# Long convolution and GEGLU layers on one core: forward transforms of two blocks by single token groups, spaced loads, a reordered opening

## The chip, the cores and the metric

The kernel runs on one core of a Trainium2 chip. The metric is the time of one execution on the device in microseconds (us); the time before is the median of three executions. A profile is a recording of one more execution. The engines are PE (TensorE, matrix multiplication into PSUM), DVE (VectorE), ACT (ScalarE), POOL (GpSimd) and SP (SyncE); each takes its own instructions in the order in which the program lists them, and semaphores join the engines. SP and POOL also issue the DMA transfers.

## What is computed

Two equal layers over x with 2048 tokens of width 576. Each adds a gated causal convolution and then a GEGLU feed-forward part with an inner width of 4608:

```python
def _A_ref(q, k, v, shift_k, ssm_k, ssm_D):
    ...                                  # k_shift: 4-tap causal filter of k
    kv = k_shift * v
    ...                                  # y: causal convolution of kv with ssm_k (2048 taps) by FFT
    y = y + kv * ssm_D[None, None, :]
    return q * y

def _B_ref(x, w_gate, w_up, w_down):
    return (_gelu(x @ w_gate) * (x @ w_up)) @ w_down

x = A_q
x = x + _A_ref(_layernorm(x, axis=-1), A_k, A_v, A_shift_k, A_ssm_k, A_ssm_D)
x = x + _B_ref(_layernorm(x, axis=-1), B_w_gate, B_w_up, B_w_down)
x = x + _A_ref(_layernorm(x, axis=-1), A_k, A_v, A_shift_k, A_ssm_k, A_ssm_D)
x = x + _B_ref(_layernorm(x, axis=-1), B_w_gate, B_w_up, B_w_down)
```

The convolution result y depends on k, v and the filters alone, so it is the same in both layers and is computed once.

## The kernel before

**Feed-forward part.** The tokens are cut into four chunks of 512 (four tiles of 128). A unit is a pair (layer, chunk); the eight units run in the order (0,0), (0,1), (1,0), (1,1), (0,2), (0,3), (1,2), (1,3), in passes of 1, 2, 2, 2 and 1 units. A pass goes through the inner width in three phases; in a phase each of its units gets one visit. A visit has 12 gu groups of 18 matmuls (L1294: gate and up projection of 128 inner columns for all 512 tokens; in the first visit L1228, by halves of the tokens) and then four dn groups, one for each token tile, of 24 matmuls of 128x288 (L1311). ACT applies the gelu to a gu group (L1298) and DVE multiplies by the up half (L1299, hT). DVE adds a dn group into the residual x_c (L1342 in the last phase of a unit, L1347 otherwise). Three PSUM buffers (pool "pr") serve the gu and dn groups in turn.

**Between units.** When a dn group ends a unit of layer 0, or a convolution result arrives, the next statistics follow for each token tile: mean to nm on POOL (L924), square sums on ACT (L932), then ve and rstd on POOL (L939, L940). For the convolution DVE gates (L960: (x - mean) times y) and adds to the residual (L967: rstd times that, plus x). For the feed-forward input DVE normalises (L993, with a copy L995), and SP issues two transposing DMAs (L1023) which write the tile into xnT. A gu matmul reads all 512 tokens of xnT, so the first gu of a unit needs all four tiles.

**Convolution by blocks.** The 2048 tokens are four blocks of 512. Block b's filter part and kv are each transformed by matmuls to four coefficient tiles kt = 0..3, each a pair s = 0, 1 of parts (128 coefficients by 576 columns); y of block m comes from products of kv block a with filter block m - a (L234, L237, L238 on DVE), sums over a (L467, L470 and L252), and an inverse transform of four matmul groups of eight (L276), whose results ACT evicts (L282). Filter and kv coefficients go to DRAM (L286) and are loaded again by POOL when their products are due (kr, L402; hr, L410). Sources of a transform are four token groups i = 0..3 of 128 rows.

- `fwd_full` (L202, matmuls L207): one coefficient tile and one s, all columns: eight matmuls of 128x288, one ACT eviction.
- `fwd_eo` (L211, matmuls L217): tiles kt and kt + 2 together, one s, one half of the columns: two matmuls over even token groups and two over odd ones, an ACT eviction into an "eo" tile (L220), and two DVE instructions in `cross` (L223): their sum is tile kt, their difference tile kt + 2. A transform takes eight such pieces, 32 matmuls.

`filt(b)` (L319) transforms the filters of blocks 2 and 3, `step(m)` (L356) does the work of block m with the transform of its kv. The eo tiles come from four buffers; the PSUM of transforms and inverses inside the feed-forward part is the single buffer "cps".

**The order** is fixed when the kernel is built. A class keeps estimated times of PE, DVE and ACT (constants C_...), and after each gu group, and every 8 matmuls of dn, `fill` (L1081) emits convolution work as far as these estimates allow a limit: `run_loads` (L526: DMA loads, up to two in one call), `run_v` (L535: from queue U the finishing of an eviction, from queue V the products and sums in order) and `run_p` (L553: from queue Pq the transform matmuls). HURRY (2.6) is a limit used as long as block 1's result isn't there.

**The opening** (`Conv.begin`, L607 to L804) transforms blocks 0 and 1 and makes y of block 0; `busy` (L649 calls) are matmuls without use, as are transposes on a constant (L1122) in `turn` (L297 and `head.turn`). `first_half` (L1192) then runs the first visit's gu groups on two token tiles, with gates of the others between, and `half_gu` (L1221) issues them. `h1_rest` (L576) queues the rest of the filter transform of block 1.

Of the kernel before, what the change touches and what calls it, by code (L numbers as in the profile page):

```python
# [22 lines left out]
P = 128  # L23
# [12 lines left out]
C_BF, C_TB = 0.37, 0.46  # L36
# [47 lines left out]
class Conv:  # L84
# [9 lines left out]
    def __init__(self, tc, ctx, pace, A_k, A_v, A_shift_k, A_ssm_k, A_ssm_D, ident, psp, cpsp, ypool):  # L94
# [29 lines left out]
        self.startup, self.other = True, False  # L124
        self.nps = 0
# [76 lines left out]
    def fwd_full(self, src, kt, s, dst, scale=1.0):  # L202
        nc = self.nc
        ps = self.ps()
        for n, i in enumerate((1, 2, 3, 0)):
            for h in range(2):
                nc.tensor.matmul(ps[:, h, 0:HW], lhsT=self.fwd_w(kt, s, i), rhs=src[:, i, h * HW:(h + 1) * HW],  # L207
                                 start=(n == 0), stop=(n == RT - 1))
        nc.scalar.activation(out=self.halves(dst[:, s, :]), in_=ps[:, :, 0:HW], func=ACT.Copy, scale=scale)
# [12 lines left out]

    def cross(self, eo, lo, hi):  # L223
        for dst, op in ((lo, ALU.add), (hi, ALU.subtract)):
            self.nc.vector.tensor_tensor(out=dst, in0=eo[:, 0, :], in1=eo[:, 1, :], op=op)  # L225

    def prod(self, part, K, H, dst=None):
        nc = self.nc
        pr = self.prp.tile([P, 2, self.D], BF16, tag="prod", name="prod")
        if dst is None:  # L230
            dst = self.smp.tile([P, self.D], BF16, tag="sum", name="sum")[:]
            self.npr += 1
        if part == 0:
            nc.vector.tensor_tensor(out=pr[:], in0=K[:], in1=H[:], op=ALU.mult)  # L234
# [84 lines left out]
    def filt(self, b):  # L319
        nc, t, D = self.nc, self.t, self.D  # L320
        kc, own = {}, {}

        def load():
            own["t"] = self.kvp.tile([P, RT, D], BF16, tag="v", name="hT")
            nc.gpsimd.dma_start(out=own["t"][:], in_=self.Td[b].rearrange("(p i) d -> p i d", i=RT))
            own["at"] = t.pe + 9.0
        self.L.append((lambda: max(self.fwd_at.get(b - 1, NEVER), self.td_at.get(b, NEVER)), load))

        def fwd(kt, s, h):
            def run():  # L330
                if s == 0 and h == 0:
                    for k in (kt, kt + 2):
                        kc[k] = self.kcp.tile([P, 2, D], BF16, tag="kc", name="hc")
                eo = self.fwd_eo(own["t"], kt, s, h)
                self.neo += 1
                done = t.on_act(C_EVA, t.pe + 0.49 + LAG)
                self.ps_free = done
                if (kt, s, h) == (1, 1, 1):
                    self.filt_at[b] = t.pe + 0.49
                cols = slice(h * HW, (h + 1) * HW)  # L340

                def fin():
                    self.cross(eo, kc[kt][:, s, cols], kc[kt + 2][:, s, cols])
                    self.neo -= 1
                    when = t.on_dve(2 * C_BF, done + LAG)
                    if s == 1 and h == 1:
                        for k in (kt, kt + 2):
                            self.spill(self.Hd[b][k], kc[k], when + LAG, (b, k))
                self.U.append((done + LAG, 2 * C_BF, fin))
            return run  # L350
        for kt in range(2):
            for s in range(2):
                for h in range(2):
                    self.Pq.append((lambda: max(own.get("at", NEVER), NEVER if self.neo >= N_EO else 0.0), 0.49, fwd(kt, s, h)))

    def step(self, m, kv=None, loaded=False):  # L356
# [37 lines left out]
        pairs = [(kt, a) for kt in KTS for a in range(m + 1)]  # L394

# [46 lines left out]

        def v(kt, a, part):
            def run():
                K = kc[kt] if a == m else kr[(kt, a)][1]
                slot = self.npr % N_SM
                prs[(kt, a, part)] = (slot, self.prod(part, K, hr[(kt, a)][1]))
                self.pr_free[slot] = NEVER
# [12 lines left out]
        def add(kt, a, part):  # L461
            def run():
# [9 lines left out]
                def fin(when):  # L472
                    self.pr_free[slot] = when
# [21 lines left out]
        for kt, a in pairs:  # L495
            for part in range(2):
                keys = [("ld", kt, a)] + ([("kc", kt % 2, s, h) for s in range(2) for h in range(2)] if a == m else [])
                self.V.append((lambda g=get(*keys): max(g(), self.pr_slot()), C_PR, v(kt, a, part)))
# [5 lines left out]
        for h in range(2):  # L504
            if h == 1:
                self.Pq.extend(self.between)
                self.between = []
# [18 lines left out]
    def run_loads(self):  # L526
# [4 lines left out]
        for _ in range(2):  # L531
            if self.L and self.L[0][0]() <= t.pe - 0.3:
                self.L.popleft()[1]()

    def run_v(self, limit):  # L535

        t = self.t
        if self.U and self.U[0][0] <= t.pe + 0.2 and max(t.dve, t.pe - 1.0) + self.U[0][1] <= limit:
# [14 lines left out]
    def run_p(self, other=False):  # L553
# [8 lines left out]
        free, self.other = self.ps_free, other  # L562
        run()
# [12 lines left out]
    def h1_rest(self):  # L576
        nc, t = self.nc, self.t

        def fwd(s, h):
            def run():  # L580
# [6 lines left out]
                def fin():  # L587
# [3 lines left out]
                    if s == 1 and h == 1:  # L591
                        for k in (1, 3):
                            self.spill(self.Hd[1][k], self.H1[:, k, :, :], when + LAG)
                self.U.append((done + LAG, 2 * C_BF, fin))
            return run
        def full(s):
            def run():
                self.fwd_full(self.hT1, 0, s, self.H1[:, 0, :, :])
                self.ps_free = t.on_act(C_EVA, t.pe + 0.98 + LAG)
                if s == 1:  # L600
                    self.spill(self.Hd[1][0], self.H1[:, 0, :, :], self.ps_free + LAG)
            return run
        for s in range(2):
            self.Pq.append((lambda: 0.0, 0.98, full(s)))
        self.between = [(lambda: NEVER if self.neo >= N_EO else 0.0, 0.49, fwd(s, h)) for s in range(2) for h in range(2)]

    def begin(self, head, tables):  # L607
# [4 lines left out]
        with ExitStack() as es:  # L612
# [37 lines left out]
            busy(3, self.ps())  # L650
# [11 lines left out]
            busy(2, self.ps())  # L662
# [39 lines left out]
            def h_part(b, kt, s):  # L702
# [7 lines left out]
                self.fwd_full(src, kt, s, t)  # L710
                if s == 1:
                    if b == 0:
                        self.flush(0.0)
# [33 lines left out]

            def tile(kt):
                for s in range(2):
                    h_part(0, kt, s)  # L750
                if kt == 2:
                    head.act_sq(2)
                    head.act_sq(3)
                kfwd(kt)
            tile(0)
            head.act_sum(2)
            head.act_sum(3)
            head.stats(0)
            head.stats(1)
            self.load_k(1, nc.gpsimd)  # L760
            kacc(0)
            tile(2)
            kacc(2)
            pair0(0, 0)
            tile(1)
            kacc(1)
            pair0(0, 1)
            tile(3)
# [6 lines left out]
            h_part(1, 2, 1)  # L775
# [3 lines left out]
            Y[3] = self.cpsp.tile([P, 2, 512], F32, tag="cps", name="cps")  # L779
# [4 lines left out]
            inv0(3, Y[3])  # L784
# [5 lines left out]
            head.mean(2)  # L790
            head.sq(0)
# [5 lines left out]
            head.turn(0, 24)  # L797
# [10 lines left out]
def ssm_geglu_kernel(ctx, tc, A_q, A_k, A_v, A_shift_k, A_ssm_k, A_ssm_D, B_x, B_w_gate, B_w_up,  # L808
# [291 lines left out]
    with tc.manual_schedule():  # L1100
# [91 lines left out]
        def first_half(hT):  # L1192
# [6 lines left out]
            for n in range(FP // 2):  # L1199
# [18 lines left out]
                if n > 1:  # L1218
                    fill(t.pe + C_GU + HURRY, True, True)
# [27 lines left out]
        hurry = lambda: (1, RT - 1) not in conv.y_at  # L1247
        visits = []
# [3 lines left out]
        for wb, ph, ui, first, final in visits:  # L1252
# [25 lines left out]
            if wb == 0:  # L1278
                first_half(hT)
                for n in range(FP // 2):  # L1280
# [5 lines left out]
                    fill(t.pe + C_GU + (HURRY if hurry() else LEAD), hurry(), conv.left > 0)  # L1286
            for fi in range(FP if wb else 0):
# [15 lines left out]
                fill(t.pe + C_GU + (HURRY if hurry() else LEAD), hurry(), conv.left > 0)  # L1303
            for j in range(RT):
# [18 lines left out]
                for fi in range(FP):  # L1323
# [78 lines left out]
```

## Time and profile before

| | us |
|---|---|
| median of three executions | 942.15 |
| lowest and highest of them | 941.43 and 945.15 |
| the profiled execution | 944.51 |
| its span in the trace | 942.7 |
| busy: PE / DVE / ACT / POOL | 929.8 / 565.4 / 293.0 / 140.2 |
| mean granted TensorE clock | 0.996 |

The page gives for each engine the busy time, for each group of equal instructions the line of the kernel, the engine, the operation, what goes out and in, the count, the total busy time and the mean in ns of one; behind the second bar stands the idle time of that engine right before such instructions, with what ended it. The timeline gives start, length and, in brackets, the idle time before and its releaser. The chain of waits goes back from the last instruction, each time to what released it. In the windows a clock of 1.00 is the full granted clock of TensorE.

### The profile page before, as it was taken

The numbers are of one execution on the slowest core, as the hardware profiler recorded it, in microseconds if no ns is written. First come the engines' busy times: TensorE is split into PE (matmuls) and PEld (weight loads), VectorE is DVE, ScalarE is ACT, GpSimd is POOL, SyncE is SP. The second block draws the span as 40 slices with busy tenths as digits, with TensorE's granted clock in tenths as the row PEclk, the third lists the DMA queues.
The fourth block names the chain that finished last, engine by engine and source line by source line (L and its number), as shares of the span: only waits on it lengthen the run. The fifth ranks groups of instructions, "written<-read, shape, count | busy, mean of one in ns | idle before, by whom it ended". The sixth has DMA issues, their size and how long they took to land.

```text
span 942.7 us, 19524 instructions
## 1 busy us (share of the span) xinstructions
PE 929.8 (99%) x8349; PEld 547.9 (58%) x8349; DVE 565.4 (60%) x1026; ACT 293.0 (31%) x539; POOL 140.2 (15%) x305
## 2 busy tenths in 40 slices
PE   9899999999999998999999999999999999999998
PEld 6787456564564654646546556556556556556555
DVE  5788978899887446888888333663333335423332
ACT  5763225432115323331222421441221223311211
POOL 2433003502103014031110100130000002100000
PEclk9999999999999998999999999999999999999999
DMA  9959987958725414954950720771630631786620
GB/s 256 350 160 252 206 190 146 300 131 214 185 87 121 132 51 114 183 155 117 189 199 4 152 76 26 144 149 37 134 94 1 133 94 14 133 207 150 149 67 26
DMA packets 128491, 130.27 MB, mean 138 GB/s; under 512 B 43538, under 2 KB 120339, under 8 KB 128404
## 3 DMA queue, kind: packets, MB, share of 16 engines
q1 hardware_dynamic: 119232, 93.47, 45.6%
q0 software_dynamic: 9168, 35.54, 11.2%
q8 instruction: 65, 1.06, 0.5%
q14 instruction: 22, 0.18, 0.1%
q10 hardware_dynamic: 4, 0.01, 0.0%
HBM read 107.76 MB, written 11.80 MB: 127 GB/s over the span
## 4 chain that ended last, share of the span: by engine, by line
PE 90%; issue 3%; DVE 2%; POOL 2%; DMA 1%; ACT 1%; DVEq 0%; POOLq 0%; ACTq 0%
PE gu L1294 54%; PE dn L1311 26%; PE gu L1228 3%; PE cps L217 2%; PE ps L207 1%; PE cps L276 1%; POOL rstd L940 1%; DMA out_dram<-ob 1%; PE cps L207 1%; DVE x_c L1342 1%; POOL ve L939 0%; ACT junk L932 0%; DVE x_c L967 0%; POOL nm L924 0%; PE hps L697 0%
## 5 line engine op out<-in xcount | busy, mean ns | idle before, releaser
L1294 PE MATMUL gu<-xnT,wgu 64*128 64x512 bf16 x4968 | 544.2, 377 | 5.2 <-DVE x_c L1342 4.6
L1294 PEld LDWEIGHTS <-wgu 64*128 64x128 bf16 x4968 | 245.5, 94 | 297.0 <-issue 15.7
L1298 ACT ACTIVATE ga<-gu 128x512 f32<-128x512 f32 x276 | 164.6, 597 | 525.3 <-PE gu L1294 514.6
L1299 DVE TENSOR_TENSOR hT<-ga,gu 128x512 bf16<-128x512 f32 x276 | 189.1, 685 | 214.7 <-ACT ga L1298 213.6
L1311 PE MATMUL dn<-wd,hT 128*128 128x288 bf16 x2304 | 293.8, 286 | 0.5 <-DVE ob L1320 0.5
L1311 PEld LDWEIGHTS <-hT 128*128 128x128 bf16 x2304 | 223.6, 98 | 66.1 <-issue 10.5
L1347 DVE TENSOR_TENSOR x_c<-x_c,dn 128x576 f32<-128x576 f32 x64 | 48.1, 752 | 76.2 <-PE dn L1311 75.8
L924 POOL TENSOR_SCALAR nm<-s 128x1 f32<-128x1 f32 x62 | 20.0, 322 | 308.5 <-DVE x_c L1342 174.5
L932 ACT ACTIVATE junk<-x_c,nm 128x576 bf16<-128x576 f32 x48 | 37.0, 771 | 40.9 <-POOL nm L924 40.5
L940 POOL TENSOR_TENSOR rstd<-ve,neghalf_t 128x1 f32<-128x1 f32 x62 | 38.9, 628 | 5.2
L410 POOL DMA_DIRECT2D hr<-Hd x32 | 17.3, 541 | 134.8 <-DVE prod L237 134.8
L220 ACT ACTIVATE eo<-cps 128x576 f32<-128x576 f32 x42 | 27.2, 649 | 28.4 <-PE cps L217 21.8
L238 DVE TENSOR_TENSOR sum<-prod 128x576 bf16<-128x576 bf16 x72 | 33.0, 458 | 2.5
L1333 DVE TENSOR_TENSOR ob<-x_c,dn 128x576 bf16<-128x576 f32 x15 | 11.2, 753 | 27.5 <-PE dn L1311 19.6
L1228 PE MATMUL gu<-xnT,wgu 64*128 64x256 bf16 x432 | 25.1, 269 | 0.5 <-DVE xnT L1132 0.5
L939 POOL TENSOR_SCALAR ve<-ss 128x1 f32<-128x1 f32 x62 | 18.5, 299 | 34.1 <-ACT junk L932 34.0
L1228 PEld LDWEIGHTS <-wgu 64*128 64x128 bf16 x432 | 21.0, 94 | 4.1 <-issue 2.3
L291 POOL DMA_DIRECT2D out_dram<-ob x12 | 6.7, 555 | 101.9 <-DVE ob L1333 99.3
L967 DVE SCALAR_TENSOR_TENSOR x_c<-g_t,rstd,x_c 128x576 f32<-128x576 f32 x16 | 13.0, 815 | 14.5 <-POOL rstd L940 14.4
L225 DVE TENSOR_TENSOR kc<-eo 128x288 bf16<-128x288 f32 x48 | 19.3, 451 | 2.3 <-ACT eo L220 2.3
L217 PEld LDWEIGHTS <-W 128*128 128x128 bf16 x176 | 16.7, 98 | 5.3 <-issue 1.3
L470 DVE TENSOR_TENSOR zs<-zs,sum 128x576 f32<-128x576 f32 x24 | 18.1, 754 | 0.4
(124 smaller groups left out, 520.2 us busy)
## 6 DMA issues: line engine op xcount, KB each, us to landing
wgu<-in_B_w_gate_dram SPq DMA_DIRECT2D x45, 576.0 KB, 5.6
wd<-in_B_w_down_dram SPq DMA_DIRECT2D x30, 864.0 KB, 6.4
wgu<-in_B_w_up_dram SPq DMA_DIRECT2D x45, 512.0 KB, 7.7
hr<-Hd POOLq DMA_DIRECT2D x32, 288.0 KB, 4.6
kr<-Kd POOLq DMA_DIRECT2D x24, 288.0 KB, 5.1
Kd<-kc POOLq DMA_DIRECT2D x12, 288.0 KB, 4.7
k<-in_A_k_dram POOLq DMA_DIRECT2D x3, 1008.0 KB, 9.0
wgu<-in_B_w_up_dram SPq DMA_DIRECT2D x45, 64.0 KB, 7.7
```

The costliest lines, as they stand in the source:

```text
L217: nc.tensor.matmul(ps[:, e, 0:HW], lhsT=self.fwd_w(kt, s, i), rhs=src[:, i, h * HW:(h + 1) * HW], start=(i == e), stop=(i == e + 2))
L220: nc.scalar.activation(out=eo[:], in_=ps[:, :, 0:HW], func=ACT.Copy, scale=scale)
L238: nc.vector.tensor_tensor(out=dst, in0=pr[:, 0, :], in1=pr[:, 1, :], op=ALU.subtract if part == 0 else ALU.add)
L924: nc.gpsimd.tensor_scalar(out=v["nm"][:], in0=v["s"][:], scalar1=-1.0 / D, scalar2=None, op0=ALU.mult)
L932: nc.scalar.activation(out=junk[:], in_=get_x(), func=ACT.Square, bias=v["nm"][:, 0:1], accum_out=v["ss"][:])
L940: nc.gpsimd.tensor_tensor(out=v["rstd"][:], in0=ve[:], in1=neghalf_t[:, 0:1], op=ALU.pow)
L1228: nc.tensor.matmul(pair[:, s, e * 256:(e + 1) * 256], lhsT=w[r0:r0 + HK, k, gi * P:(gi + 1) * P], rhs=xnT[r0:r0 + HK, blk_of[k], tok], sta ...
L1294: nc.tensor.matmul(pair[:, s, :], lhsT=w[r0:r0 + HK, k, gi * P:(gi + 1) * P], rhs=xnT[r0:r0 + HK, b, :], start=(k == 0), stop=(k == NKC - 1))
L1298: nc.scalar.activation(out=ga[:], in_=pair[:, 0, :], func=ACT.Gelu_apprx_tanh)
L1299: nc.vector.tensor_tensor(out=hT[:, fi, :], in0=ga[:], in1=pair[:, 1, :], op=ALU.mult)
L1311: nc.tensor.matmul(acc[:, h, 0:HW], lhsT=hT[:, fi, at * P:(at + 1) * P], rhs=wd[2 * wb + fi // WT][:, fi % WT, h * HW:(h + 1) * HW], start ...
L1347: nc.vector.tensor_tensor(out=xh, in0=xh, in1=acc[:, :, 0:HW], op=ALU.add)
```

## The change

1. `quarter` replaces the `fwd_eo` pieces for the filters and the kv of blocks 2 and 3. One half of the columns takes four pieces, one for each token group (order 0, 2, 1, 3), of two matmuls (both s); ACT evicts each into an eo buffer. DVE then forms sums and differences of groups 0 and 2 and of groups 1 and 3 in f32 (`both`), from these the tiles 0 and 2 (`even`) and 1 and 3 (`odd`).
2. `run_loads` issues one load in a call, at least 0.5 us of estimated PE time behind the last, and at least 1.6 us while statistics are queued for DVE or ACT. `run_v` does nothing when the head of U doesn't fit.
3. Block 1's products go in another order of (kt, a), and some use a buffer of their own in place of a sum slot; they wait for the filter tiles' finishing (h1_at).
4. The opening: filter tiles 0 and 2 of block 0 as one even/odd pair with `cross`, three useless matmuls become one and two others go, 24 useless transposes become 8, some ACT and statistics steps stand later, one transform of block 1 stands behind the gates with its eviction on DVE, and two further tile transforms of block 1's filter are taken between the kv transforms.
5. `first_half` takes no convolution matmuls, dn calls `fill` with HURRY's limit while block 1's result isn't there, and C_BF is 0.41 in place of 0.37.

```diff
+    def quarter(self, src, out, h, ready, seen, done):
...
+        def both(a, b):
+            tt(out=A[b][:], in0=A[a][:], in1=A[b][:], op=add)
+            nc.vector.scalar_tensor_tensor(out=A[a][:], in0=A[a][:], scalar=2.0, in1=A[b][:], op0=ALU.mult, op1=sub)
+            t.on_dve(2 * C_R4)
+
+        def even():
+            for kt, op in ((0, add), (2, sub)):
+                tt(out=out()[kt][:, :, cols], in0=A[2][:], in1=A[3][:], op=op)
+            done(0, h, t.on_dve(2 * C_R4) + LAG)
+
+        def odd():
+            for kt, ops in ((1, (add, sub)), (3, (sub, add))):
+                for s in range(2):
+                    tt(out=out()[kt][:, s, cols], in0=A[0][:, s, :], in1=A[1][:, 1 - s, :], op=ops[s])
+            self.neo -= RT
+            done(1, h, t.on_dve(4 * C_BF) + LAG)
+
+        def one(i):
+            def run():
+                ps = self.ps()
+                for s in range(2):
+                    nc.tensor.matmul(ps[:, s, 0:HW], lhsT=self.W[:, 2 * i + s, :], rhs=src()[:, i, cols], start=True, stop=True)
+                A[i] = self.eop.tile([P, 2, HW], F32, tag="eo", name="eo")
+                nc.scalar.copy(out=A[i][:], in_=ps[:, :, 0:HW])
+                self.neo += 1
...
+                if i == 2:
+                    self.U.append((when + LAG, 2 * C_R4, lambda: both(0, 2)))
+                if i == 3:
+                    seen(h)
+                    self.U.append((when + LAG, 2 * C_R4, lambda: both(1, 3)))
+                    self.U.append((when + LAG, 2 * C_R4, even))
+                    self.U.append((when + LAG, 4 * C_BF, odd))
+            return run
+        return [(lambda i=i: max(ready(), NEVER if self.neo >= (N_EO if i else 1) else 0.0), 0.25, one(i)) for i in (0, 2, 1, 3)]
...
         pairs = [(kt, a) for kt in KTS for a in range(m + 1)]
+        if m == 1:
+            pairs = [(kt + (2 * e if a else 2 - 2 * e), a) for kt in range(2) for a in range(2) for e in range(2)]
...
+            if m > 1:
+                self.Pq.extend(self.quarter(lambda: self.vt_[m], out4, h, get(("kv", h)), seen4, done4))
+                continue
...
-        for _ in range(2):
-            if self.L and self.L[0][0]() <= t.pe - 0.3:
-                self.L.popleft()[1]()
+        gap = 1.6 if self.tight() else 0.5
+        if self.L and self.L[0][0]() <= t.pe - 0.3 and t.pe - self.load_at >= gap:
+            self.load_at = t.pe
+            self.L.popleft()[1]()
...
-            busy(3, self.ps())
+            busy(1, self.ps())
...
-            busy(2, self.ps())
...
+            def h0_pair(s, h):
...
+                eo = self.fwd_eo(hT0, 0, s, h)
+                cols = slice(h * HW, (h + 1) * HW)
+                self.cross(eo, h0[0][:, s, cols], h0[2][:, s, cols])
...
-            tile(0)
+            for s in range(2):
+                for h in range(2):
+                    h0_pair(s, h)
+            kfwd(0)
...
-            tile(2)
+            kfwd(2)
...
             h_part(1, 2, 0)
-            h_part(1, 2, 1)
...
+            h_part(1, 2, 1, nc.vector.tensor_copy, small())
...
+            Y[3] = inv0(3, small())
...
-            head.turn(0, 24)
+            head.turn(0, 8)
...
-                    fill(t.pe + C_GU + HURRY, True, True)
+                    fill(t.pe + C_GU + HURRY, False, True)
...
+        conv.tight = lambda: bool(vq or aq)
...
-                        fill(t.pe + 1.5, True, conv.left > 0)
+                        fill(t.pe + (HURRY if hurry() else 1.5), True, conv.left > 0)
```

More of the change, by code (lines that the diff above doesn't have):

```diff
@@ L327, in filt, with out, seen, done @@
         self.L.append((lambda: max(self.fwd_at.get(b - 1, NEVER), self.td_at.get(b, NEVER)), load))
[L329 to L354, printed above, removed]
+        def out():
+            if not kc:
+                self.flush(NEVER)
+                kc.update({k: self.kcp.tile([P, 2, D], BF16, tag="kc", name="hc") for k in range(RT)})
+            return kc
+        def seen(h):
+            if h == 1:
+                self.filt_at[b] = t.pe + 0.25
+        def done(kt, h, when):
+            if h == 1:
+                for k in (kt, kt + 2):
+                    self.spill(self.Hd[b][k], kc[k], when, (b, k))
+        for h in range(2):
+            self.Pq.extend(self.quarter(lambda: own["t"], out, h, lambda: own.get("at", NEVER), seen, done))
     def step(self, m, kv=None, loaded=False):
@@ L1302, in ssm_geglu_kernel @@
                     when_due(t.pe + (FP - FG) * C_GU + 12.0, load_wgu, n + 3)
-                fill(t.pe + C_GU + (HURRY if hurry() else LEAD), hurry(), conv.left > 0)
+                fill(t.pe + C_GU + (HURRY if hurry() else LEAD), now(), conv.left > 0)
             for j in range(RT):
```

100 lines of the change are left out of this document (68 added, 32 removed).

## The prediction

> **What bounds the kernel now.** I read the page's shares first, then its chain of work that ended last and its costliest groups.
>
> ```profile
> PE 929.8 (99%) x8349; PEld 547.9 (58%) x8349; DVE 565.4 (60%) x1026; ACT 293.0 (31%) x539; POOL 140.2 (15%) x305
> ...
> PE 90%; issue 3%; DVE 2%; POOL 2%; DMA 1%; ACT 1%; DVEq 0%; POOLq 0%; ACTq 0%
> ...
> L1294 PE MATMUL gu<-xnT,wgu 64*128 64x512 bf16 x4968 | 544.2, 377 | 5.2 <-DVE x_c L1342 4.6
> L220 ACT ACTIVATE eo<-cps 128x576 f32<-128x576 f32 x42 | 27.2, 649 | 28.4 <-PE cps L217 21.8
> L225 DVE TENSOR_TENSOR kc<-eo 128x288 bf16<-128x288 f32 x48 | 19.3, 451 | 2.3 <-ACT eo L220 2.3
> L470 DVE TENSOR_TENSOR zs<-zs,sum 128x576 f32<-128x576 f32 x24 | 18.1, 754 | 0.4
> L967 DVE SCALAR_TENSOR_TENSOR x_c<-g_t,rstd,x_c 128x576 f32<-128x576 f32 x16 | 13.0, 815 | 14.5 <-POOL rstd L940 14.4
> ```
>
> The matmul engine is busy 929.8 of 942.7 us and 90% of the last chain. So a matmul taken away anywhere shortens the run by its spacing, and an engine that feeds PE matters only where it makes PE wait: 12.9 us in all now. The spacings come from the chain of waits, whose pieces are start, length, what:
>
> ```profile
> 90.57 23.42 PE gu L1294 x216
> 113.99 11.87 PE dn L1311 x96
> ...
> 154.88 0.98 PE dn L1311 x8
> 156.35 0.98 PE dn L1311 x8
> ...
> 365.60 22.24 PE gu L1294 x180
> ```
>
> A gu matmul takes 23.42 / 216 = 0.108 us, a dn matmul 11.87 / 96 = 0.124. At 154.88 a transform piece of four matmuls stands between two groups of eight dn: 156.35 - 154.88 - 0.98 = 0.49 for four, 0.1225 each, and nothing is lost around it.
>
> **The one large stall** is at 361 to 372 us, at the end of unit (0,1). Timeline (start, length, engine, operation, idle before), then windows of PE with the granted clock behind the busy time:
>
> ```profile
> 349.30 0.76 DVE L1342 SCALAR_TENSOR_TENSOR x_c<-dn,x_c 128x576 f32<-128x576 f32 x1 [1.26 <-PE dn L1311]
> ...
> 358.93 0.63 POOL L402 DMA_DIRECT2D kr<-Kd  x1
> ...
> 362.60 0.54 POOL L410 DMA_DIRECT2D hr<-Hd  x1
> ...
> 364.04 0.82 DVE L967 SCALAR_TENSOR_TENSOR x_c<-g_t,rstd,x_c 128x576 f32<-128x576 f32 x1 [4.27 <-POOL rstd L940]
> ...
> 365.60 1.89 PE L1294 MATMUL gu<-xnT,wgu 64*128 64x512 bf16 x8 [3.60 <-DVE x_c L1342]
> ```
>
> ```profile
> 360.00:362.00 2.00, 2.00 (x20) 1.00 0.84 161
> 362.00:364.00 2.00, 0.00 (x0) 1.00 1.12 303
> 364.00:366.00 2.00, 0.40 (x3) 0.54 1.02 369
> ...
> 368.00:370.00 2.00, 2.00 (x12) 0.50 0.72 144
> 370.00:372.00 2.00, 2.00 (x18) 0.76 0.02 4
> ```
>
> Six loads (three kr, three hr) are issued on POOL ahead of two rstd; DVE waits 4.27 us in L967, behind it stands the L1342 that empties PE's PSUM buffer, and PE is idle 3.60 us. Then the clock is at 0.50, with twelve matmuls in 2 us where the free rate gives 18. The chain's piece from 365.60 shows what that costs: 180 matmuls in 22.24 us against 180 x 0.108 = 19.5, so 2.7, and I use 2.8 with the gap ahead. Idle and clock: 6.4. The same boundary later, without loads in the way:
>
> ```profile
> 610.46 0.76 DVE L1342 SCALAR_TENSOR_TENSOR x_c<-dn,x_c 128x576 f32<-128x576 f32 x1 [1.73 <-PE dn L1311]
> 613.38 0.82 DVE L967 SCALAR_TENSOR_TENSOR x_c<-g_t,rstd,x_c 128x576 f32<-128x576 f32 x1 [1.00 <-POOL rstd L940]
> ...
> 618.30 0.58 DVE L993 TENSOR_SCALAR xn<-x_c,nm,rstd 128x576 bf16<-128x576 f32 x1
> ...
> 618.91 0.18 DVE L995 COPY xn<-xn 128x64 bf16<-128x64 bf16 x1
> 618.99 0.78 ACT L932 ACTIVATE junk<-x_c,nm 128x576 bf16<-128x576 f32 x1 [2.81 <-POOL nm L924]
> ...
> 619.12 2.53 SPq L1023 DMA_TRANSPOSE xnT<-xn  x2
> ...
> 619.67 0.19 ACT L932 ACTIVATION_READ_ACCUMULATOR junk<-x_c,nm 128x1 f32 x1
> ...
> 623.72 1.47 PE L1294 MATMUL gu<-xnT,wgu 64*128 64x512 bf16 x12 [0.49 <-DVE x_c L1342]
> ```
>
> It costs 0.5, call it 0.6 with the issue gaps.
>
> **The change, part by part,** summed against the profiled execution's span of 942.7.
>
> *Transforms of blocks 2 and 3.* Four transforms (two filters, two kv) go from 32 to 16 matmuls each: 64 x 0.1225 = **-7.8**, all on PE's path. ACT still evicts four times per half (0.649 each). DVE pays: per half it did eight L225 adds (0.451 each: 3.6); now two tensor_tensor and two scalar_tensor_tensor on 128x576 f32 (0.754 and 0.815), two more of the first for the even tiles (f32 in, bf16 out; taken at the same 0.754) and four of L225's kind: 3.1 + 1.5 + 1.8 = 6.4. That is 2.8 us more, 22 over eight halves. They lie beside PE's gu and dn groups; where DVE is full I come back to it as a rival.
>
> *Buffers of a half.* Four eo buffers hold exactly one half, and the first piece of the next stands, at three places of the new order, right behind the four odd adds that free them. Each time the second piece, with the single cps buffer, is late by about one eviction (0.649): **+2.0**; nothing if DVE is early, 3 if it lags a further instruction.
>
> *Spaced loads.* In the new order no load stands between the statistics of that boundary, so the 6.4 become 0.6: **-5.8**, between -3 (clock stays, half the wait) and -6.4. A load that comes later is late next for a product; those have some tens of us.
>
> *Block 1's products* keep their number and their operations; only pairs and buffers change: 0. They are hidden under the gu groups, and block 1's inverse stays more than a whole dn group (11.87) ahead of its user.
>
> *Opening.* Block 0's filter tiles 0 and 2 as one even/odd pair take 16 matmuls away, and one transform of block 1 steps behind the gates:
>
> ```profile
> 34.78 0.98 PE cps L207 x8
> ...
> DVE prod L234 <- ACT kc L209: 4.2, 3, 2.5
> ...
> 44.51 1.71 PE L1228 MATMUL gu<-xnT,wgu 64*128 64x256 bf16 x26 [0.45 <-DVE xnT L1132]
> ```
>
> (chain, waits, timeline). Best case: 16 x 0.1225 = 1.96 and 0.98, -2.9. But eight DVE crosses (8 x 0.451 = 3.6) come in; the 4.2 us that DVE waits there for ACT would hide them if they fell in it. If none does: 3.6 - 2.9 = +0.7. I take **-1.0**, a little nearer to the bad end, as the wait comes in three pieces. The four filling matmuls and 16 of 24 filling transposes that go stand in PE's waits: 0.
>
> *A new wait at the end of unit (0,0).* In the new order the first piece of block 2's filter stands in the last third of this unit's dn, and its eviction stands on ACT behind the square of the second token tile's result. Above, that square starts 618.99 - 610.46 = 8.5 us after the first L1342, which starts 0.1 us after the first 24 dn end. The piece ends 50 dn and two transform matmuls, 6.4 us, after that point; PE goes on for 8 dn (1.0) and stands at the second piece, which needs cps: 8.6 + 0.78 + 0.19 (its accumulator read) + 0.65 + gaps of 0.3 against 7.4: **+3.2**. Bounds 0 (ACT ahead) and 3.2 + 2.8 if the clock falls as it did after 3.60. Behind the eviction ACT has only more squares; behind PE the gelu starts later by as much.
>
> *A new wait at unit (0,3).* Block 3's inverse moves from two visits ahead of its user to the dn groups right before it: 64 dn, 64 x 0.124 = 7.9 us, lie between its last matmul and the first gu, which needs all four token tiles gated, normalised and transposed. Before, that chain ran unhurried:
>
> ```profile
> 587.28 0.81 DVE L960 SCALAR_TENSOR_TENSOR x_c<-x_b,nm,y 128x576 f32<-128x576 bf16 x1
> ...
> 594.82 11.64 SPq L1023 DMA_TRANSPOSE xnT<-xn  x8
> ...
> xnT<-xn SPq DMA_TRANSPOSE x56, 2.6
> ```
>
> From the first gate to the last landing: 594.82 + 11.64 - 587.28 = 19.2, and 2.6 (issue to landing) less 1.3 for the last one's own issue: 20.5. In the new order the first gate follows the first inverse piece's eviction, 0.9 after that piece; from there to the gu stand 3 inverse pieces (24 x 0.1225) and 94 dn: 14.6 - 0.9 = 13.7. Late by 6.8; with eight transposes back to back (8 x 1.26 = 10.1 in place of 11.64) 5.3; if only the last tile's chain counted (eviction 0.65, gate 0.82, residual and statistics 2.9 as from 610.46 to 613.38, norm 0.58 + 0.18, two transposes 1.3 + 2.6, six hand-overs of 0.1: 9.6) 1.7. I take 6.5 idle, and the clock's 2.8 behind it, as after the 3.60; the 0.6 of the old boundary is in it: **+8.7**, from 1.1 to 9.0.
>
> The granted clock fell after 3.60 idle. The Trainium skill (TensorE: Matmul & The Clock Gate, Part 1: The HAM clock gate) says that the gate halves the rate after one idle window of about 3.4 us, counted freely, and frees it after as long a busy one. The rows at 364 to 372 agree (0.54, 0.50, 0.50, 0.76). By it the 3.2 at unit (0,0) would mostly stay below the window and the 6.5 would not, as I took them; a window that fell badly would make the sum 2.8 worse.
>
> Sum: -7.8 + 2.0 - 5.8 - 1.0 + 3.2 + 8.7 = **-0.7**. The profiled execution took 944.51 with its 942.7 span, at the upper side of 941.43 to 945.15; on the median of 942.15 it gives 941.4. I say **941**.
>
> **The rivals.**
> 1. *The waits are short*: the evictions come in time at (0,0), and at (0,3) only the last tile's chain counts, without a drop of the clock. For it: DVE and ACT have little else in dn. Against: eight transposes follow each other on one queue. -7.8 + 2.0 - 5.8 - 1.0 + 0 + 1.1 = -11.5: 930.6.
> 2. *Slower: VectorE becomes the bound.* Where the transforms stand it has little left (windows: PE, PEld, DVE, ACT, POOL busy, clock, DMA share, GB/s):
>
> ```profile
> 210.00:300.00 90.00, 90.00 (x807) 48.25 (x804) 76.95 (x136) 25.96 (x50) 16.48 (x29) 1.00 0.59 149
> ...
> 400.00:520.00 120.00, 120.00 (x1066) 66.67 (x1066) 103.58 (x187) 30.15 (x58) 19.53 (x40) 1.00 0.51 134
> ```
>
> 103.58 of 120 in the last; half of the 22 us more makes 114.6. If the last half's work (6.4) doesn't fit, PE stands that long at block 3's inverse, ahead of the wait at (0,3): 941.4 + 6.4 = 947.8. It decides against the kernel from 5.5 us on. Against it: block 3's products have two visits more than before.
> 3. *The spaced loads don't mend unit (0,1)*, since the statistics are late by themselves: +5.8, 947.2. Against it: the boundary at 610 to 624.
>
> **How the numbers follow.** This kernel's measurement tells 0.5% (4.7 us) from no change: faster is under 937.4, slower over 946.9. The forecast .43 (its clock drops and the eo waits spread it by some 5: faster .11, same .28, slower .04); short waits .28 (faster .27, same .01); VectorE .19 (same .04, slower .15); loads .10 (same .05, slower .05). Together .38, .38, .24. The range reaches down below the short waits by the rest of the opening (-1.9) to 929, and up past VectorE by a further lag to 949; the likeliest case alone is 936 to 946.
>
> **What would show it.** 8 or so us less of transform matmuls with DVE's busy time up by about 22 to 26; no PE wait of 3.6 at the end of unit (0,1) and clock 1.00 there; at the end of unit (0,0) a wait of PE's transform piece on ACT's eviction near 3 us; at unit (0,3)'s first gu a wait near 6.5 on a transpose, with the clock at 0.50 behind it. Wrong would be: neither wait there (then 931), or waits of gu groups on hT or of products all through 150 to 520 (then DVE bounds).

## The result and the profile after

| | before | changed |
|---|---|---|
| median of 8 executions, us | 944.85 | 936.87 |
| lowest to highest | 941.04 to 945.86 | 935.61 to 939.49 |
| span of the profiled execution | 942.7 | 934.9 |

The ratio is 0.9932 with a 95% interval of 0.9912 to 0.9953: the changed kernel is faster by 0.7%. The median of before, 942.15 from three executions when the prediction was written, is 944.85 with eight. The kernel before runs in two groups, at 941.0 to 942.2 us with a mean clock of 1.000 and at 943.3 to 945.9 with 0.996 to 0.998, so the half clock behind its stall comes in a part of the executions only; the profiled one has it.

The page of the changed kernel, its shares and the chain:

```profile
PE 917.5 (98%) x8248; PEld 536.7 (57%) x8249; DVE 589.0 (63%) x1051; ACT 291.9 (31%) x538; POOL 143.5 (15%) x305
...
PE 93%; DVE 3%; POOL 2%; issue 1%; ACT 1%; DMA 0%; SPq 0%; DVEq 0%
...
L1376 PE MATMUL gu<-xnT,wgu 64*128 64x512 bf16 x4968 | 544.0, 377 | 5.9 <-DMA xnT<-xn 5.4
```

PE's busy time falls by 12.3 us, DVE's rises by 23.6, and the gu groups now wait for a transpose (5.4 us) where they waited for DVE (4.6). PE still bounds the run. Where the time went is read from a ledger, which compares each start of a gu or dn group with what PE's work up to there takes at the free rate (0.108 and 0.124 us for each gu and dn matmul, 0.1225 for a conv matmul). First the end of unit (0,1), where before stood the 3.60 us; this is its part of the chain (start, length, what):

```profile
298.42 11.87 PE dn L1393 x96
310.29 23.42 PE gu L1376 x216
333.71 11.87 PE dn L1393 x96
345.57 23.42 PE gu L1376 x216
```

Each group follows the last with no gap: the 6.4 us are gone. Then the end of unit (0,0), the timeline:

```profile
153.37 0.76 DVE L1424 SCALAR_TENSOR_TENSOR x_c<-dn,x_c 128x576 f32<-128x576 f32 x1 [1.43 <-PE dn L1393]
...
159.29 0.41 PE L254 MATMUL cps<-hT,W 128*128 128x288 bf16 x2
...
162.17 0.78 ACT L1012 ACTIVATE junk<-x_c,nm 128x576 bf16<-128x576 f32 x1 [2.81 <-POOL nm L1004]
...
162.94 0.62 ACT L256 COPY eo<-cps 128x576 f32<-128x576 f32 x1
...
163.61 0.40 PE L254 MATMUL cps<-hT,W 128*128 128x288 bf16 x2 [2.93 <-ACT eo L256]
```

The first filter piece ends at 159.7, its eviction starts at 162.94 behind the square at 162.17, and PE stands 2.93 us at the second piece. The square starts 8.8 us after the first L1424 (153.37); 8.5 was assumed. Last the first gu of unit (0,3), timeline, chain and windows (PE busy, granted clock):

```profile
596.31 8.00 PE L1393 MATMUL dn<-wd,hT 128*128 128x288 bf16 x64
...
598.46 10.62 SPq L1103 DMA_TRANSPOSE xnT<-xn  x8
...
605.52 0.58 DVE L1073 TENSOR_SCALAR xn<-x_c,nm,rstd 128x576 bf16<-128x576 f32 x1 [2.56 <-POOL rstd L1020]
...
606.14 0.18 DVE L1075 COPY xn<-xn 128x64 bf16<-128x64 bf16 x1
...
609.27 0.61 PE L1376 MATMUL gu<-xnT,wgu 64*128 64x512 bf16 x2 [4.95 <-DMA xnT<-xn]
```

```profile
610.34 25.91 PE gu L1376 x214
```

```profile
608.00:610.00 2.00, 0.61 (x2) 0.72 0.63 125
610.00:612.00 2.00, 1.66 (x8) 0.50 0.72 159
612.00:614.00 2.00, 2.00 (x12) 0.50 1.06 380
614.00:616.00 2.00, 2.00 (x12) 0.57 0.99 329
616.00:618.00 2.00, 2.00 (x22) 1.00 0.08 25
```

PE is idle 4.95 us, then 214 matmuls take 25.91 us where 23.2 are due: 2.7 for the clock. Two things are late by nearly the same. The last tile's norm starts at 605.52, since DVE waits 2.56 us for its rstd, which stands in POOL's row of statistics of two units; its copy is done at 606.32. And the eight transposes follow each other: at 1.26 us each (their median) they fill 10.1 of the 10.62 us. The sixth, from the timeline of SP alone:

```profile
605.18 1.27 SPq L1103 DMA_TRANSPOSE xnT<-xn  x1
```

It ends at 606.45, 0.1 us after that copy, and only then can the last tile's two start. By these rows an earlier norm of the last tile alone would have gained 0.1 us at most.

### The profile page after: what moved, and what is told of

Same layout as the page of the kernel before. It is cut to its first block, busy times and chain, and to the rows that moved or that the text cites. A ratio compares the mean times of both kernels' runs of the same rounds, so it can differ in the third digit from the quotient of the medians.

```text
span 934.9 us, 19345 instructions
## 1 busy us (share of the span) xinstructions
PE 917.5 (98%) x8248; PEld 536.7 (57%) x8249; DVE 589.0 (63%) x1051; ACT 291.9 (31%) x538; POOL 143.5 (15%) x305
## 4 chain that ended last, share of the span: by engine, by line
PE 93%; DVE 3%; POOL 2%; issue 1%; ACT 1%; DMA 0%; SPq 0%; DVEq 0%
PE gu L1376 58%; PE dn L1393 28%; PE gu L1308 3%; PE cps L325 1%; PE cps L254 1%; POOL rstd L1020 1%; PE cps L219 1%; DVE x_c L1424 0%; POOL ve L1019 0%; DVE yb L287 0%; ACT junk L1012 0%; POOL nm L1004 0%; DVE prod L286 0%; PE ps L209 0%; DVE yb L799 0%
## 5 line engine op out<-in xcount | busy, mean ns | idle before, releaser
L1004 POOL TENSOR_SCALAR nm<-s 128x1 f32<-128x1 f32 x62 | 24.6, 397 | 299.3 <-DVE x_c L1424 170.2
L256 ACT COPY eo<-cps 128x576 f32<-128x576 f32 x32 | 20.4, 637 | 31.6 <-PE cps L254 31.6
L287 DVE TENSOR_TENSOR prod<-prod 128x576 bf16<-128x576 bf16 x48 | 22.0, 458 | 1.7
L1073 DVE TENSOR_SCALAR xn<-x_c,nm,rstd 128x576 bf16<-128x576 f32 x28 | 16.1, 576 | 4.5 <-POOL rstd L1020 4.4
L529 DVE TENSOR_TENSOR zs<-zs,prod 128x576 f32<-128x576 f32 x24 | 18.1, 754 | 0.3
L526 DVE TENSOR_TENSOR zs<-sum,prod 128x576 f32<-128x576 bf16 x24 | 18.1, 753 | 0.3
L184 DVE TENSOR_TENSOR kvt<-k,skc 128x1152 bf16<-128x1152 bf16 x24 | 17.7, 753 | 0.2
```

The costliest lines, as they stand in the source:

```text
L256: nc.scalar.copy(out=A[i][:], in_=ps[:, :, 0:HW])
L526: nc.vector.tensor_tensor(out=f[:], in0=self.halves(pr0[:]), in1=self.halves(pr[:]), op=ALU.add)
L1004: nc.gpsimd.tensor_scalar(out=v["nm"][:], in0=v["s"][:], scalar1=-1.0 / D, scalar2=None, op0=ALU.mult)
```

## The experiments

The first four and two later ones take the change apart: "transforms" are `quarter` (and its two users), "loads" is the spaced `run_loads`, and "opening" all the rest (opening, block 1's order, the new rule in `run_v`, fill limits and C_BF). Two of the eight combinations are the kernels known so far; the other six were run, all against the kernel before.

**The transforms alone**, added to the kernel before:

```diff
+            if m > 1:
+                self.Pq.extend(self.quarter(lambda: self.vt_[m], out4, h, get(("kv", h)), seen4, done4))
+                continue
...
```

> The kernel before with only the four-piece transforms of blocks 2 and 3. Theory: 64 matmuls fewer, -7.8 us of span. In its order the first filter piece stands 33 dn matmuls ahead of where the changed kernel has it, so its eviction is ahead of the squares at the end of unit (0,0): no wait of PE on an eviction over 1 us; and block 3's inverse stands a whole visit ahead of unit (0,3): no wait on a transpose there. No load stands between the statistics at the end of unit (0,1) either: another -6. Span about 929 against 942.7, ratio near 0.985. Rival (VectorE is the bound, or the pieces themselves bring the waits): waits of 3 and 5 us as in the changed kernel come here too, span 937 to 941.

Measured: 933.61 (ratio 0.9903, 0.9884 to 0.9922), span 933.0. No wait on an eviction is over 1.24 us, and there is none on a transpose; of the stall at the end of unit (0,1) 1.4 are left. The span is 4 us over the expectation: at the end of unit (1,0), DVE stood 6.25 us because a buffer of the output was still being stored, and PE 2.17 us behind it, with the half clock after that. The timeline and the windows there:

```profile
392.14 0.75 DVE L1388 TENSOR_TENSOR ob<-x_c,dn 128x576 bf16<-128x576 f32 x1 [6.25 <-DMA out_dram<-ob]
392.94 23.23 PE L1349 MATMUL gu<-xnT,wgu 64*128 64x512 bf16 x198 [2.17 <-DVE ob L1388]
```

```profile
392.00:394.00 2.00, 1.06 (x10) 1.00 1.02 399
394.00:396.00 2.00, 2.00 (x14) 0.57 1.08 387
396.00:398.00 2.00, 2.00 (x14) 0.58 1.08 368
```

By the ledger this place costs 4.0 us, so about 1.9 of them are the clock, behind a gap of only 2.17 us.

So the transforms bring neither of the two new waits by themselves, and the extra DVE work isn't the bound.

**The changed kernel without the spacing:**

```diff
-        gap = 1.6 if self.tight() else 0.5
-        if self.L and self.L[0][0]() <= t.pe - 0.3 and t.pe - self.load_at >= gap:
-            self.load_at = t.pe
-            self.L.popleft()[1]()
+        for _ in range(2):
+            if self.L and self.L[0][0]() <= t.pe - 0.3:
+                self.L.popleft()[1]()
```

> The changed kernel with the load pacing of before (up to two loads in a call, no spacing). Theory: the spacing is what puts block 3's inverse right before unit (0,3); without it the inverse stands a visit earlier, the wait of 5.0 us on the transpose and the half clock behind it (together 8) go; the filter pieces at the end of unit (0,0) stand 4 us earlier but still beside the squares, so 1 to 3 us of wait on an eviction stay. Span 926 to 929 against 934.9. Rival (the extra DVE work puts it late): the wait at unit (0,3) stays, span 934 to 936. Second rival (unspaced loads bring the 3.6 us stall at the end of unit (0,1) back): a wait on L1424's kind there and 6 us more, span 933.

Measured: 930.76 (0.9877, 0.9862 to 0.9892), span 929.3, against 936.87: 6 us faster without the spacing. Block 3's inverse stands a whole visit earlier, and unit (0,3) starts with no more than the old boundary's wait. The chain:

```profile
563.00 0.98 PE cps L325 x8
...
569.61 0.98 PE cps L325 x8
...
571.33 23.42 PE gu L1375 x216
594.74 3.06 PE dn L1392 x24
...
611.10 19.60 PE gu L1375 x180
```

At the end of unit (0,0) 1.65 us stay of the 3.1, at the end of (0,1) stand 1.4, and 1.2 are new at the end of (1,0): the stall of before doesn't come back. The theory holds, 0.3 us above its range; both rivals fall.

**The opening and the rest alone** (the changed kernel with both other parts taken back):

> The changed kernel with the old transforms and the old load pacing, so the new opening, the new product order of block 1 and the fill limits alone. Theory: 3.4 us earlier at the first gu group, as in the changed kernel, and no load between the statistics of unit (0,1) by its order: -3.4 - 6 to span 933; no 5 us wait at unit (0,3), whose inverse stands 40 us of PE ahead. Rival (the stall at the end of unit (0,1) is not the loads'): -3.4 alone, span 939.

Measured: 945.73 (1.0029, 1.0012 to 1.0046), span 943.3: slower than before, and neither theory had that. The first gu is 2.2 us earlier (42.30), the stall at unit (0,1) is 1.5, but at the end of unit (1,0) the store of an output holds DVE and a transform piece:

```profile
396.26 0.76 DVE L1421 TENSOR_TENSOR ob<-x_c,dn 128x576 bf16<-128x576 f32 x1 [7.52 <-DMA out_dram<-ob]
...
397.75 1.14 PE L219 MATMUL cps<-v,W 128*128 128x288 bf16 x4 [4.65 <-DVE v L194]
```

With the clock behind it that costs 7.3 us; 1.6 more stand at the end of unit (0,0).

**The spaced loads alone**, added to the kernel before:

> The kernel before with the spaced loads alone. Theory: the six kr and hr loads leave the statistics at the end of unit (0,1); the 4.27 us wait of L967, PE's 3.60 us and the half clock go: -6, span 936 to 937. Rival (the statistics are late by themselves): span 942 to 943.

Measured: 942.19 (0.9998, 0.9984 to 1.0012), span 939.4. The wait of 3.60 and its half clock are gone, but 1.9 us appear at the end of unit (0,0) and 2.0 at the end of (0,1), where transform pieces now wait for evictions:

```profile
350.02 0.65 PE L218 MATMUL cps<-hT,W 128*128 128x288 bf16 x4 [0.62 <-ACT eo L221]
...
359.10 0.65 PE L218 MATMUL cps<-hT,W 128*128 128x288 bf16 x4 [0.58 <-ACT eo L221]
```

The stall is mended, but 3.9 of its 6.4 us come back at these two places, and the timed runs show no difference.

**The clock behind the wait at unit (0,3).** Useless matmuls on PE right before the first gu:

```diff
+                if (layer, c, ph, fi) == (0, 3, 0, 0):
+                    for _ in range(32):
+                        nc.tensor.matmul(pair[:, 0, 0:288], lhsT=ident[:], ...)
                 for k in range(NKC):
```

> The changed kernel with 32 matmuls of 128x288 without use (32 x 0.1225 = 3.9 us) put on PE right before the first gu group of unit (0,3), into the PSUM buffer that this group then overwrites. The chain that PE waits for there is untouched, so the first gu starts as late as before. Theory (the 2.7 us that its 216 matmuls lose behind the wait are the clock, halved because PE stood idle 5 us): idle falls to about 1 us, the clock stays 1.00, and the group takes 23.4 in place of 25.9 + its start: span 2.7 less, about 932. Rival (the half clock has another cause, or the useless matmuls delay the group): span unchanged or up to 4 us more.

The timeline and the windows:

```profile
605.67 4.08 PE L1375 MATMUL gu<-W,ident 128*128 128x288 bf16 x32
611.35 0.39 PE L1380 MATMUL gu<-xnT,wgu 64*128 64x512 bf16 x2 [1.60 <-DMA xnT<-xn]
612.42 23.27 PE L1380 MATMUL gu<-xnT,wgu 64*128 64x512 bf16 x214 [0.68 <-DMA xnT<-xn]
```

```profile
610.00:612.00 2.00, 0.39 (x2) 1.00 0.68 134
612.00:614.00 2.00, 1.58 (x16) 1.00 0.67 168
```

The same 214 matmuls take 23.27 in place of 25.91, at a clock of 1.00: the 2.64 us are the clock, and here it falls because PE stands. The span of about 932 that the theory gave didn't come: it is 934.3, the median 936.04 against 936.87. In this profiled execution the opening was 1.5 us later (first gu at 42.66), and the first gu of (0,3) came 0.7 us later after its dn.

**The old transform for block 3's kv only**, in the changed kernel:

```diff
-            if m > 1:
+            if m == 2:
                 self.Pq.extend(self.quarter(lambda: self.vt_[m], out4, h, get(("kv", h)), seen4, done4))
```

> The changed kernel, spaced loads and all, with the old eight-piece transform for the kv of block 3 alone: 16 matmuls more on PE (+2.0 us), some 5 us of DVE work less ahead of block 3's products. By its order block 3's inverse then stands a whole visit ahead of unit (0,3). Theory (the wait at (0,3) hangs only on where the inverse stands, and 5 us of DVE work are enough to tip it): the wait and the clock, 8 us, go: 934.9 + 2.0 - 7.9 = 929. Rival (the wait is in the statistics of the units there): 937.

Measured: 931.82 (0.9873, 0.9852 to 0.9893), span 929.6. The wait at (0,3) and its clock are gone, the 2.9 at (0,0) stays. Sixteen matmuls more make the kernel 5 us faster, since block 3's inverse then stands a visit earlier.

**Transforms and spaced loads on the old opening:**

> The kernel before with the four-piece transforms and the spaced loads, old opening. By its order block 3's inverse stands a visit ahead of unit (0,3) and the filter pieces at the end of unit (0,0) as early as in the kernel with the transforms alone (933.0). Theory: the spacing is harmful only where it moves those; here it does not, so the span is within 3 us of 933.0. Rival (spacing costs by itself, through later products): 938 or more.

Measured: 934.24 (0.9900, 0.9877 to 0.9924), span 934.8: as the transforms alone.

**The opening and the spaced loads with the old transforms:**

> The changed kernel with the old eight-piece transforms: new opening and spaced loads. Its PE order is that of the kernel with the opening alone (943.3, which lost 6 us at the end of unit (1,0) where a transform piece waited 4.6 us on DVE, which waited 7.5 us for an output store to free its buffer). Theory: one load later by a third of a us does not mend that: span 941 to 944. Rival (the six loads ahead of the output stores are what makes them late, and spacing helps): 4 to 6 us less, 937 to 939.

Measured: 946.53 (1.0035, 1.0011 to 1.0058), span 946.7: 2.7 us over the theory. At the end of (1,0) stand 6.1 us, as without the spacing (6.0), and at the end of unit (0,0) 4.3, where without it stood 1.6. All eight together, medians in us:

| | loads as before | spaced loads |
|---|---|---|
| old transforms, old opening | 943.7 to 944.9 | 942.2 |
| new transforms, old opening | 933.6 | 934.2 |
| old transforms, new opening | 945.7 | 946.5 |
| new transforms, new opening | 930.8 | 936.9 |

Spacing costs 6 us in one place of four and gains nothing clear in any; the opening costs 2 to 4 us with the old transforms; with the new ones it gains 3 without the spacing and costs 3 with it. The entries come from several rounds, between which the median of the kernel before differs by 1 us.

**The filter's pieces earlier**, in the changed kernel with its spacing:

```diff
-                        self.td_at[b] = t.pe + 9.0
-                    self.late.append((t.pe + 14.0, out))
+                        self.td_at[b] = t.pe + 7.0
+                    self.late.append((t.pe + 10.0, out))
...
-            own["at"] = t.pe + 9.0
+            own["at"] = t.pe + 7.0
```

> The changed kernel, spaced loads and all, with three assumed delays of the filter's path shortened (its spill to DRAM 10 in place of 14 us of estimated PE time after its transposes, the load 7 in place of 9 after the spill, the transform 7 in place of 9 after the load). Nothing else is edited. By its order the four filter pieces move from the last quarter of the dn groups that end unit (0,0) to their first third, ahead of the squares, and block 3's inverse stands a visit earlier. Theory (both new waits come from where these pieces stand, not from the pieces, the DVE work or the spacing as such): no wait of 2.9 us on the eviction, none of 5.0 on the transpose, clock 1.00: 934.9 - 3.1 - 7.9 = 924, up to 927 with the 1.4 and 1.2 us that the kernel without spacing lost at 351 and 390 us. Rival (the load lands later than the shortened delay says): PE waits for the filter's DMA at about 151 us instead, up to 5 us, span 927 to 932.

Measured: 931.33 (0.9871, 0.9848 to 0.9894), span 928.4. Both waits are gone; in place of the first PE stands 1.8 us for a transpose at the next gu, which was in neither theory and puts the span 1.4 above the expected range. With 11, 8 and 8:

> As the kernel with the early filter, with delays of 11, 8 and 8 us: the first filter piece stands 34 dn matmuls into the dn groups at the end of unit (0,0), against 2 there and 74 in the changed kernel. Theory: no wait for the DMA; the evictions meet the squares of the first token tile, so 1 to 2 us of wait on them stay; block 3's inverse is a visit early, no wait at (0,3): span 925 to 928. Rival (waits on evictions do not hang on where the pieces stand): 3 us there, 928 to 929.

Measured: **929.40** (0.9846, 0.9829 to 0.9864), span 928.0, the lowest median of all and faster than both kernels (against the changed kernel without the spacing the intervals overlap). The end of unit (0,0):

```profile
155.03 0.41 PE L254 MATMUL cps<-hT,W 128*128 128x288 bf16 x2
...
155.37 0.78 ACT L1012 ACTIVATE junk<-x_c,nm 128x576 bf16<-128x576 f32 x1 [3.00 <-POOL nm L1004]
...
156.15 0.62 ACT L256 COPY eo<-cps 128x576 f32<-128x576 f32 x1
...
156.81 0.41 PE L254 MATMUL cps<-hT,W 128*128 128x288 bf16 x2 [0.40 <-ACT eo L256]
```

The eviction meets a square here too, but one that starts at once: 0.40 us in place of 2.93, and 0.9 in all at this boundary; at (0,3) PE has no wait on a transpose. Three numbers of an estimate moved a few matmuls by 5 us, and that undid both waits. (The edit shortens the delays of block 3's filter as well; no run moves one filter alone.)

**The useless matmuls of the opening put back:**

> The changed kernel with the four useless matmuls at the start put back. The recorded prediction costed them at nothing. Theory now (two of them stood on PE's path ahead of the first transposes of k, 0.97 us at 5.33 in the chain of before): those transposes start about 1 us later (5.8 in place of 4.78), and the first gu group up to 1 us later, 42.1 in place of 41.14; span up to 1 us more. Rival (they lie in PE's waits): the same start within the 1 us by which the first gu differs between executions of one opening.

Measured: 938.19 (0.9935, 0.9918 to 0.9952), span 936.6; the ratio is that of the changed kernel (0.9932), so the timed runs show no difference. The chains of the changed kernel and of this one, in this order:

```profile
4.78 2.39 PE kps L743 x20
...
41.14 6.21 PE gu L1308 x108
```

```profile
6.29 2.27 PE kps L744 x20
...
42.75 6.21 PE gu L1309 x108
```

The first transposes start 1.5 us later with them. The first gu is 1.6 later, but other kernels with the new opening start it between 41.02 and 42.66, so how much of the 1.5 arrives there stays open.

## Why the prediction was right in its range, and 4 us high

The 936.87 lies in the range of 929 to 949, at the low edge of the 936 to 946 that was given to the likeliest case. The change itself was missed by more: 0.7 us less were forecast, and 7.8 came in the span. The distance in time is smaller by luck, because the median of three that the 941 was put on is 2.7 us below that of eight. Of the mechanisms, the transforms and the two new waits came as described; the eo step did not happen, the opening was mis-sized, and the end of unit (0,1) has another cause than the one named.

| step | predicted | measured in the profiled executions |
|---|---|---|
| 64 transform matmuls | -7.8 | -7.8 |
| eo buffers of a half | +2.0 | 0 |
| stall at the end of unit (0,1) | -5.8 | -6.4 |
| opening | -1.0 | -3.8 |
| wait at unit (0,0) | +3.2 | +3.1 |
| wait and clock at unit (0,3), less 0.6 | +8.7 | +7.9 |
| a wait of 0.6 and its gap at 834 us that didn't come | not named | -0.8 |
| sum | -0.7 | -7.8 |

The measured column is the difference of the two ledgers at the starts of the groups: 7.84 us of PE work less for the transforms and 3.76 for the opening, +3.09 at (0,0), 8.51 - 0.66 at (0,3), -6.41, -0.79.

- **Transforms:** right. 64 matmuls of L254 stand where 128 of L217 stood, and DVE's busy time rises by 23.6, for which 22 to 26 was named.
- **eo buffers:** wrong. At the three places the dn groups take their own time: from 189.39 to 202.48 are 13.09 us for 96 dn (11.87) and five pieces of 0.245 (1.2). The next half's first piece stands there:

```profile
196.86 1.55 DVE L246 TENSOR_TENSOR hc<-eo 128x288 bf16<-128x288 f32 x4
197.66 0.41 PE L254 MATMUL cps<-hT,W 128*128 128x288 bf16 x2
...
198.11 0.64 ACT L256 COPY eo<-cps 128x576 f32<-128x576 f32 x1 [7.45 <-PE cps L254]
...
198.89 0.41 PE L254 MATMUL cps<-hT,W 128*128 128x288 bf16 x2
```

  Its eviction starts 0.45 us after it, as those behind it do, and waited for PE; the second piece follows eight dn later without a wait. The four odd adds (L246) were through at 198.41, ahead of the second eviction at 199.34. The step took the order of the list for lateness and had no row for it.
- **Unit (0,1):** the size was right, the cause was not. The prediction gave it to the spaced loads. The spacing does remove the stall when it is alone, but so do the new transforms and the new opening without it: any of them moves the six loads away from those statistics. In the changed kernel the spacing is worth +6 us, not -5.8.
- **Opening:** mis-sized. It is the largest error, and even its best case (-2.9) was passed. The bound of +0.7, for adds that fall into no wait, didn't come near: the eight adds stand where the kernel before took statistics (from 15.96 us on) and then waited for ACT, and those statistics moved behind the first products, where DVE had stood 2.51 us for ACT. Rows of the kernel before, then of the changed kernel:

```profile
19.74 0.76 DVE L234 TENSOR_TENSOR prod<-kc,h 128x1152 bf16<-128x1152 bf16 x1 [1.26 <-ACT kc L209]
...
24.73 0.76 DVE L234 TENSOR_TENSOR prod<-kc,h 128x1152 bf16<-128x1152 bf16 x1 [2.51 <-ACT kc L209]
```

```profile
15.10 3.04 DVE L272 TENSOR_TENSOR h<-eo 128x288 bf16<-128x288 f32 x8 [0.27 <-ACT eo L222]
18.52 0.76 DVE L283 TENSOR_TENSOR prod<-kc,h 128x1152 bf16<-128x1152 bf16 x1 [0.38 <-ACT kc L211]
```

  The first product starts at 18.52 even with the adds ahead of it, and the products behind it have no wait for ACT. The useless work, costed at nothing, may be a part as well: it is worth 1.5 us at the first transposes, and how much of that reaches the first gu stays open. The 3.8 is that of one execution: over all profiled ones the first gu stands at 44.0 to 45.0 with the old opening (mean 44.5) and 41.0 to 42.7 with the new (mean 41.9), so up to there the opening is worth about 2.6. What each of its parts is worth no run shows.
- **Unit (0,0):** right, to 0.1 us, by the chain of the old boundary at 610 us (its terms add up to 3.1, not 3.2). That the clock held behind it was not sure, as the last paragraph of this section shows.
- **Unit (0,3):** right within 0.8. The idle time was 5.0 for 6.5 taken, and the clock 2.7 for 2.8. The value of 5.3, for eight transposes back to back, would have been the better one, and back to back is what they did. It was put down to the order of the whole change; the runs show what in the order: the filter's load waits its turn under the spacing, its pieces come 4 us later, and from there each half of a transform stands later until block 3's inverse slips by one visit. That the slip follows from the filters' delays is shown by the early filter; that it runs through block 2's pieces, and by which of the later steps, was read from the order alone. It can be undone later too: with block 3's old kv transform the filter's pieces stay late and the slip is gone.
- **Rivals:** VectorE as the bound falls: no gu group waits on hT, and unit (0,1) stays mended. The short waits came only in the kernels that move the pieces.

The Trainium skill (TensorE: Matmul & The Clock Gate, Part 1: The HAM clock gate) puts the fall of the clock after an idle window of about 3.4 us. Some gaps here fit it: 2.93 us at (0,0) left the clock at 1.00 in all four profiled executions that have it, the 4.95 at (0,3) was followed by 0.50, and with that gap filled to 1.60 and 0.68 the clock stayed at 1.00. Three shorter gaps don't fit. Behind 2.17 us (transforms alone) and 2.10 us (transforms and spaced loads) at the end of unit (1,0) the clock was 0.57 and 0.50 in the lowest stretch of 2 us, and behind 2.70 us at (0,0) with the old transforms it was 0.55. So the length of a gap alone doesn't tell here whether the clock falls, and that it held behind the 2.93 was in part luck; what else decides, no run shows.

## What to carry to other kernels

A stall that is gone isn't yet the work of the edit that was meant to remove it: run each part alone and the whole without each part. In a kernel whose order comes from estimated times, delays assumed 1 to 3 us too long can shift a whole chain of work by a visit; look for the first instruction that moved and try the estimate there before the parts that wait in the end. And a stall of PE can cost the half clock behind it as well, here 1.9 us behind a gap of 2.17 and 2.7 behind 3.60 and 4.95.

## What the runs showed of the hardware that was not expected

- A DVE instruction that writes an output buffer waited 4.75 to 7.62 us for that buffer's earlier store, at the end of unit (1,0) in six of the kernels; being in order, DVE held products, the hT multiplies and PE behind it. With old transforms and new opening it cost 7 to 8 us with the clock, more than any other wait of those kernels.
- The same opening started the first gu group at 41.02 to 42.66 us in eight profiled executions of the changed kernel and its variants. Differences of 1 us between single executions say nothing about an edit of the opening.
- The clock of TensorE fell to half behind gaps of 2.10, 2.17 and 2.70 us and stayed full behind 2.93 us.
